# Gate and value products of a DeltaNet + SwiGLU kernel: eleven half-chunk products instead of twelve (Strassen's scheme), with weight sums streamed from DRAM

## The chip, the cores and the metric

The kernel runs on one core of one Trainium2 chip. The metric is the device time of one execution in microseconds (us); lower is better. All arithmetic and all data on the chip are 32-bit floats.

The engines are named as the profile names them: PE is the matrix engine (PEld its weight loads, which overlap its matmuls), DVE the vector engine, ACT the scalar engine, POOL the GpSimd engine, and SP the queue from which nearly all DMA transfers are issued. Every engine works through its own queue in order. [...]

## The reference

Two blocks follow each other. The first is a recurrent attention (DeltaNet); its output, regrouped to 3072 tokens of 384 features, is the input of a SwiGLU block.

```python
# q, k, v: (4, 8, 768, 48), beta: (4, 8, 768)
k_n = k / (np.linalg.norm(k, axis=-1, keepdims=True) + 1e-06)
state = np.zeros((B, H, D, D))
for t in range(S):
    y[:, :, t] = einsum('bhd,bhde->bhe', q[:, :, t], state)
    v_old = einsum('bhde,bhd->bhe', state, k_n[:, :, t])
    state = state + beta_t * einsum('bhd,bhe->bhde', k_n[:, :, t], v_t - v_old)
x = y.transpose(0, 2, 1, 3).reshape(B * S, H * D)          # 3072 x 384
g = x @ w_gate                                             # 384 -> 1536
out = (g * (1 / (1 + np.exp(-g))) * (x @ w_val)) @ w_out   # 1536 -> 384
```

## The kernel before, in words

The 768 time steps are cut into 12 chunks (`NCH`) of 64 steps. With four batches, a chunk has 256 tokens (`TOK`). For each chunk the attention makes a tile `xts[c]` of 3 x 128 features by 256 tokens, and the SwiGLU block then consumes it:

- `gate_val(c, f)` makes two blocks of 128 hidden units (`f` and `f+1`) of gate and of value. Each is a sum over three feature tiles (`t`), with 128 x 128 weights as the stationary operand and all 256 tokens as the moving operand. `p_gate` and `p_val` fill one PSUM bank each, and four banks rotate through `ps_ffn`. ACT forms `sil` = silu(`p_gate`), DVE multiplies it by `p_val` into a hidden tile `h_f`. It is called six times per chunk.
- `output_fast(c)`, from chunk 3 on (`FAST`), makes the output product with Strassen's scheme: 7 products for 8 on two halves of the hidden units, tokens and output columns. Some of its weight sums were put in place of weights that are no longer needed (`combos`), and `sums_of_h` makes sums of hidden tiles on DVE.

Chunks 0 to 2 use the plain `output`. Their weights arrive while they run: `convert` turns the inputs' 64-bit words into 32-bit floats.

The attention of the next chunk is woven into this stream of matmuls by hand, in program order:

- `point(c + 1)` emits the next small step for chunk c+1 or a later one: one of the four steps of `advance` (the recurrence, with 64 x 64 matmuls; the second step also loads `vin`, the third `kn`), a step of `products` (first the DVE transposes of k and q in `turned`, with the loads of the next blocks, then the Gram products in `gram`), or a step of `join`.
- `fill(n)` emits up to n steps of `invert(g)`, the inversion of a pair of chunks' 32 x 32 triangles on DVE. It opens with three transposes (`turn`), has one operation on POOL for which two calls are skipped (`WAIT`), goes on with 31 steps of two vector operations (`substitute`, lines 488 and 494), and closes with three more transposes and some small ones.
- `finish(c + 1)` emits whatever is left of the next chunk's steps at the end of a chunk.

So for each chunk the program has a fixed sequence: `point`, then six times [`gate_val` with `fill(2)`, `point`, `fill(3)`], then the output with `fill` and `point` between its products.

Of the kernel before, what the change touches and what calls it, by code (L numbers as in the profile page):

```python
# [20 lines left out]
def kernel(  # L21
# [51 lines left out]
    def ps_ffn(shape, name):  # L73
        return psum.tile(shape, FP32, name=name, tag="ffn", bufs=4)
# [9 lines left out]
    last_k = const.tile([128, 2 * KW], FP32, name="last_k")  # L84
    knp.append(last_k[:, 0:KW])
    kts.append(last_k[:, KW : 2 * KW])
    knp = [t.rearrange("p (bp h d) -> p bp h d", bp=NB, h=H) for t in knp]

    def slot(c):
        return c if c < AHEAD else (c - AHEAD) % (AHEAD - 1)  # L90

    def freed_by_k(c):

        return c - AHEAD if c < 2 * AHEAD - 1 else c - AHEAD + 1
# [21 lines left out]
    def load_k(c, dmas=(nc.sync,)):  # L116
        for n in range(2 * NB):
            bp, b = divmod(n, 2)
            dmas[n % len(dmas)].dma_start(  # L119
                out=knp[slot(c)][64 * b : 64 * b + 64, bp, :, 0:D],  # L120
                in_=halves(k, c, bp, b).rearrange("h p d -> p h d"),
            )
# [10 lines left out]
    K_BLOCKS, Q_BLOCKS = 6, 3  # L133
# [88 lines left out]
    def stage(n):  # L222
        _, src, t, f0, m = pieces[n]
        name, lo = place_of[n]
        if name not in places:
            tag_bufs = {"zb": 1, "p_sb": 2}[name]
            places[name] = work.tile(
                [128, 2 * PIECE], U32, name="staged", tag=name, bufs=tag_bufs
            )
        place = places[name][:, lo : lo + 2 * m]  # L230
        staged[n] = place
        nc.sync.dma_start(
            out=place, in_=src[t * 128 : (t + 1) * 128, f0 : f0 + m].bitcast(U32)
        )
# [71 lines left out]

    state = const.tile([128, 2, NB, NJ, D], FP32, name="state")
# [80 lines left out]
    def turned(c, of_q, tag=None):  # L388

        tag = tag or ("py" if of_q else "px")  # L390
        x = qpad[c % QB] if of_q else knp[slot(c)]
        if of_q:
            xt = work.tile([128, NB * NJ * 2 * C], FP32, name="qt", bufs=1)
        else:
            xt = kts[slot(c)]
        if c >= blocks_of[of_q][1]:
            xt_v = xt.rearrange("p (bp b j i) -> p bp j b i", bp=NB, b=2, j=NJ)
            (qt if of_q else kt)[c] = xt_v
            blocks = blocks_of[of_q][2]
            nc.vector.transpose(xt, blocks.rearrange("p bp h d -> p (bp h d)"))  # L400
            if c + 1 < NCH:
                load_blocks(of_q, c + 1)
            return
        xt = xt.rearrange("p (bp j b i) -> p bp j b i", bp=NB, j=NJ, b=2)
        (qt if of_q else kt)[c] = xt
        p_t = banks("p_t", tag)
        for bp in range(NB):
            for j in range(NJ):
                at = slice(128 * j, 128 * j + 128)
                nc.tensor.transpose(p_t[bp][:, at], x[:, bp, 2 * j : 2 * j + 2], ident)  # L410
        for bp in range(NB):
            nc.scalar.copy(xt[:, bp].rearrange("p j b i -> p (j b i)"), p_t[bp])
        if of_q and c + QB < Q_BLOCKS:
            load_q(c + QB)

    def gram_steps(c, of_q, tag=None, copies=(nc.vector.tensor_copy,) * 2):
# [10 lines left out]
        if of_q:  # L427
            p_sb[c] = work.tile([128, 2, NB, NJ, C], FP32, name="p_sb", bufs=2)
        elif c % 2 == 0:
            a = work.tile([128, C * 2 * HH], FP32, name="a_sb")  # L430
            a_sb[c // 2] = a.rearrange("p (c h i) -> p c h i", c=2, h=HH)
            a_of[c // 2] = a
# [139 lines left out]
    def late_z(g, zb):  # L572

        nc.vector.transpose(
            ztp[g % ZB].rearrange("p c h i -> p i (c h)")[:, R:C],
            zb.rearrange("p k i -> p i k"),
        )
        yield
        z_late[g] = work.tile([128, R, 2 * HH], FP32, name="d_t", tag="p_sb", bufs=2)
        nc.vector.transpose(z_late[g], zb)  # L580
        yield
# [126 lines left out]
    def advance(c):  # L708

        kn = knp[slot(c)]  # L710
# [58 lines left out]
        def of_state():  # L769
# [14 lines left out]
            for later in range(AHEAD, NCH):  # L784
                if freed_by_k(later) == c:
                    load_k(later)
# [29 lines left out]
    hs = {}  # L816

    def gate_val(c, f, fill, within=None, behind=None):

        ps = {}  # L820
        for w_sb, name in ((wg_sb, "p_gate"), (wv_sb, "p_val")):
            ps[name] = ps_ffn([128, 2, TOK], name)
            for i in range(2):
                for t in range(KT):
                    nc.tensor.matmul(  # L825
                        ps[name][:, i],
                        w_sb[:, t, (f + i) * 128 : (f + i + 1) * 128],
                        xts[c][:, t],
                        start=(t == 0),
                        stop=(t == KT - 1),  # L830
                    )
            if name == "p_gate":
                sil = ffn_pool.tile([128, 2, TOK], FP32, name="sil", bufs=1)
# [4 lines left out]
        at = len(hs) if c < 2 else (len(hs) - 12) % 8  # L838
        hs[c, f] = hp[at].rearrange("p (i n) -> p i n", i=2)
        nc.vector.tensor_tensor(out=hs[c, f], in0=sil, in1=ps["p_val"], op=ALU.mult)  # L840
        if c >= FAST:
            if f >= FT // 2:
                sums_of_h(c, f)
            elif combos:
                combos.pop(0)()
# [4 lines left out]
    def output(c, bp, fill, between=()):  # L850
        p_o = ps_ffn([128, DM], "p_o")
# [46 lines left out]

    def minus_t4():
        minus(w_t4[0], w_quarter(1, 0)[:, 0 : FH - 2], w_t2[:, 0 : FH - 2])  # L900
        minus(w_t4[1], w_quarter(1, 0)[:, FH - 2 : FH], w_t2[:, FH - 2 : FH])
# [28 lines left out]
    def output_fast(c, fill):  # L930

        p = {}

        def product(x, part, a, b):
            begun = (x, part) in p
            if not begun:
                p[x, part] = ps_ffn([128, DH], "p_o")
# [10 lines left out]
        def add(out, a, b):  # L948
            nc.vector.tensor_tensor(out=out, in0=a, in1=b, op=ALU.add)  # L949

# [3 lines left out]
        o = [new_o() for _ in range(NB)]  # L954
        left, right = slice(0, DH), slice(DH, DM)
        product(0, 0, lambda f: h_of(c, f, 0), quarter(0, 0))
        nc.scalar.copy(o[0][:, right], p[0, 0])
        product(0, 1, lambda f: s_of(2, f), lambda f: w_t2[:, f])
        add(o[0][:, right], o[0][:, right], p[0, 1])
        fill(2)  # L960
        product(1, 0, lambda f: h_of(c, f, 1), lambda f: w_t3[:, f])
        add(o[1][:, right], o[0][:, right], p[1, 0])
# [7 lines left out]
        add(o[1][:, right], o[1][:, right], p[1, 1])  # L970
# [7 lines left out]
        add(o[1][:, left], o[0][:, right], p[1, 0])  # L978
        store(c, 1, o[1])
        product(1, 1, lambda f: h_of(c, f + FH, 0), quarter(1, 1))  # L980
        add(o[0][:, right], o[0][:, right], p[1, 1])
        store(c, 0, o[0])
        fill(7)
# [25 lines left out]
    def products(k_c, q_c):  # L1009
# [6 lines left out]
        if k_c is not None:  # L1016
            copies = nc.scalar.copy if k_c < 6 else nc.vector.tensor_copy
            gram(k_c, False, None, (copies, copies))
# [24 lines left out]

    def prep_step(c):
# [17 lines left out]
        elif not (c > 0 and hold and not todo and k_of and steps("advance", freed_by_k(k_of[0])) >= 4):  # L1062
            return False
        if k_of and steps("advance", freed_by_k(k_of[0])) >= 4:
# [49 lines left out]
    with tc.manual_schedule(  # L1114
# [120 lines left out]
        for c in range(2, NCH):  # L1235
            point(c + 1)
            for f in range(0, FT, 2):
                gate_val(c, f, fill, behind=c + 1)
            if c >= FAST:
                output_fast(c, fill)  # L1240
            else:
                output(c, 0, fill)
                point(c + 1)
                output(c, 1, fill)
            finish(c + 1)

# [29 lines left out]
```

## Time and profile before

| | us |
|---|---|
| median of 8 runs | 735.09 (734.15 to 736.3) |
| the profiled execution: its time | 734.88 |
| the profiled execution: span from first to last instruction | 733.0 |
| PE busy, and share of the span | 697.2 (95%) |
| PE weight loads busy | 604.0 (82%) |
| DVE busy | 447.8 (61%) |
| ACT busy | 167.3 (23%) |
| POOL busy | 51.9 (7%) |
| mean granted PE clock | 0.966 |

The profile is one execution, recorded by the hardware. In its group rows a line of the source, an engine, an operation and its tiles stand first, then the shape and the count; after the bar come the busy time, the mean duration of one instruction in ns, and the idle time of the engine before them. Matmuls overlap in a pipeline, so the mean duration of one is longer than the distance from one to the next; the distance is read from the timeline or from the chain of waits. A matmul call of the kernel on 32-bit data appears as two pairs of weight load and matmul: the 72 calls of line 825 in each of the 12 chunks stand as 864 + 864 instructions. A transpose on PE (lines 410 and 805) is one pair.

### The profile page before, as it was taken

Reading aid. Unit: us, or ns where it says so; the run is one execution under the profiler, and the core shown is the slowest. Engines: PE = TensorE matmul, PEld = TensorE weight load, DVE = VectorE, ACT = ScalarE, POOL = GpSimd, SP = SyncE. Lnnn points to the kernel's source line nnn. Section 1 sums busy time; section 2 is a strip of 40 time slices with the busy share of each in tenths; the row PEclk is TensorE's granted clock in tenths of the full one; section 3 lists DMA queues with packets and bytes.
Section 4 is the critical chain, followed back from the end, with each engine's and each line's share of the span. In section 5 each row is a group of like instructions: output and inputs, shape, how many; then the busy total and the mean of one; then the engine's idle time right before and its main releaser. Section 6 shows DMA issues by size and latency. Waiting matters only on the chain.

```text
span 733.0 us, 22491 instructions
## 1 busy us (share of the span) xinstructions
PE 697.2 (95%) x10132; PEld 604.0 (82%) x10132; DVE 447.8 (61%) x904; ACT 167.3 (23%) x323; POOL 51.9 (7%) x46
## 2 busy tenths in 40 slices
PE   4657999999999999999999999999999999999997
PEld 3545888856787789988888988888988988989987
DVE  5995766697598162769853669853669853313122
ACT  3477654202401202021012021012011012021010
POOL 7003000203000000030000030000030000000000
PEclk9557999999999999999999999999999999999999
DMA  7786453210231112422102332202211000000000
GB/s 148 169 236 175 107 138 115 36 31 16 54 46 24 23 23 45 61 51 37 30 3 46 42 70 29 38 3 43 46 25 23 22 3 3 22 3 0 23 1 21
DMA packets 130736, 37.19 MB, mean 51 GB/s; under 512 B 122864, under 2 KB 125936, under 8 KB 130640
## 3 DMA queue, kind: packets, MB, share of 16 engines
q1 hardware_dynamic: 127184, 34.01, 23.0%
q10 hardware_dynamic: 3072, 1.57, 1.0%
q8 instruction: 79, 1.29, 0.8%
q0 software_dynamic: 384, 0.17, 0.1%
q14 instruction: 17, 0.14, 0.1%
HBM read 31.01 MB, written 4.72 MB: 49 GB/s over the span
## 4 chain that ended last, share of the span: by engine, by line
PE 81%; DVE 7%; SPq 3%; DMA 3%; ACT 3%; issue 2%; ACTq 0%; DVEq 0%
PE p_gate L825 24%; PE p_val L825 24%; PE p_o L939 14%; PE p_o L856 6%; PE p_g L422 2%; DVE tmp L488 2%; PE p_r L720 2%; PE p_u L741 2%; DVE zb L494 2%; PE p_s L772 1%; PE p_y L760 1%; PE p_y L729 1%; DMA zt<-in_moe_w_gate_dram 1%; SPq L127 1%; SPq L119 1%
## 5 line engine op out<-in xcount | busy, mean ns | idle before, releaser
L825 PE MATMUL p_gate<-x_ffn,wg_sb 128*128 128x256 f32 x864 | 204.5, 387 | 1.3 <-ACT x_ffn L808 1.3
L825 PE MATMUL p_val<-x_ffn,wv_sb 128*128 128x256 f32 x864 | 198.6, 379 | 0.0
L825 PEld LDWEIGHTS p_val<-x_ffn,wv_sb 128*128 128x128 f32 x864 | 163.8, 190 | 22.3
L825 PEld LDWEIGHTS p_gate<-x_ffn,wg_sb 128*128 128x128 f32 x864 | 161.2, 191 | 24.1 <-ACT x_ffn L808 1.8
L840 DVE TENSOR_TENSOR h_f<-sil,p_val 128x512 f32<-128x512 f32 x71 | 48.5, 684 | 158.5 <-PE p_val L825 156.7
L834 ACT ACTIVATE sil<-p_gate 128x512 f32<-128x512 f32 x72 | 43.0, 597 | 294.8 <-PE p_gate L825 273.1
L939 PE MATMUL p_o<-wo_sb,h_f 128*128 128x192 f32 x432 | 75.7, 328 | 1.0 <-DVE o_sb L949 0.9
L939 PEld LDWEIGHTS p_o<-wo_sb,h_f 128*128 128x128 f32 x432 | 70.2, 190 | 2.4 <-DVE o_sb L949 1.9
L488 DVE TENSOR_TENSOR tmp<-zb,mb 128x31 f32<-128x31 f32 (+15 forms) x186 | 63.4, 341 | 12.3 <-PE p_j L608 6.7
L494 DVE TENSOR_TENSOR zb<-zb,tmp 128x31 f32<-128x31 f32 (+15 forms) x186 | 63.7, 343 | 6.4
L633 POOL TENSOR_TENSOR n_b<-mb,half 128x32 f32<-128x32 f32 x5 | 28.1, 5628 | 412.2 <-DVE mb L458 372.7
L949 DVE TENSOR_TENSOR o_sb<-o_sb,p_o 128x192 f32<-128x192 f32 x45 | 15.6, 350 | 53.0 <-PE p_o L939 35.9
L856 PE MATMUL p_o<-wo_sb,h_f 128*128 128x384 f32 x136 | 45.7, 490 | 0.0
L856 PEld LDWEIGHTS p_o<-wo_sb,h_f 128*128 128x128 f32 x136 | 25.3, 190 | 16.5
L939 PE MATMUL p_o<-last_k,h_f 128*128 128x192 f32 x180 | 32.7, 328 | 1.1 <-DVE o_sb L949 1.1
L939 PEld LDWEIGHTS p_o<-last_k,h_f 128*128 128x128 f32 x180 | 29.6, 190 | 2.0 <-DVE o_sb L949 1.7
L897 DVE TENSOR_TENSOR h_f<-h_f,h_f 128x256 f32<-128x256 f32 x54 | 22.4, 424 | 8.0 <-PE p_o L939 7.1
L939 PE MATMUL p_o<-last_h,h_f 128*128 128x192 f32 x144 | 26.3, 326 | 0.0
L939 PEld LDWEIGHTS p_o<-last_h,h_f 128*128 128x128 f32 x144 | 23.9, 190 | 0.0
L741 PEld LDWEIGHTS p_u<-vin,zt 64*64 64x64 f32 x768 | 13.7, 141 | 5.6 <-issue 3.2
L458 DVE STREAM_TRANSPOSE mb<-a_sb 32x1024 f32<-32x1024 f32 x8 | 17.0, 2126 | 0.2
L752 ACT COPY uu<-p_u 128x768 f32<-128x768 f32 (+1 forms) x13 | 9.7, 750 | 31.7 <-PE p_u L741 31.7
(180 smaller groups left out, 681.3 us busy)
## 6 DMA issues: line engine op xcount, KB each, us to landing
vin<-in_v_dram SPq DMA_DIRECT2D x96, 48.0 KB
kn<-in_k_dram SPq DMA_DIRECT2D x40, 96.0 KB
out_dram<-o_sb SPq DMA_DIRECT2D x36, 96.0 KB
zt<-in_moe_w_out_dram SPq DMA_DIRECT2D x6, 384.0 KB
staged<-in_moe_w_out_dram SPq DMA_DIRECT2D x6, 384.0 KB
qpad<-in_q_dram SPq DMA_DIRECT2D x36, 64.0 KB
wo_sb<-in_moe_w_gate_dram SPq DMA_DIRECT2D x4, 512.0 KB
wo_sb<-in_moe_w_val_dram SPq DMA_DIRECT2D x4, 512.0 KB
```

Source lines behind the costliest of these rows:

```text
L458: nc.vector.transpose(out(rows, 0), in_(rows, 0))
L488: nc.vector.tensor_tensor(out=t_v, in0=zb[:, 0 : j + 1, j : j + 1].to_broadcast([128, j + 1, m]), in1=mb[:, j : j + 1, j + 1 : R].to_broad ...
L494: nc.vector.tensor_tensor(out=zb[:, 0 : j + 1, j + 1 : R], in0=zb[:, 0 : j + 1, j + 1 : R], in1=t_v, op=ALU.add,)
L633: nc.gpsimd.tensor_tensor(out=n, in0=mb.rearrange("p j i -> p (j i)")[:, 0 : R * R : R + 1], in1=half, op=ALU.pow,)
L741: nc.tensor.matmul(p_u[half_of(b), par, bp, j], zt[half_of(b ^ par), par, bp, j], r[half_of(b ^ par), par, bp, j], start=first, stop=True, ...
L825: nc.tensor.matmul(ps[name][:, i], w_sb[:, t, (f + i) * 128 : (f + i + 1) * 128], xts[c][:, t], start=(t == 0), stop=(t == KT - 1),)
L834: nc.scalar.activation(sil, ps[name], ACTF.Silu)
L840: nc.vector.tensor_tensor(out=hs[c, f], in0=sil, in1=ps["p_val"], op=ALU.mult)
L856: nc.tensor.matmul(p_o, hs[c, f - f % 2][:, f % 2, bp * 128 : (bp + 1) * 128], wo_sb[:, f], start=(f == 0), stop=(f == FT - 1),)
L897: nc.vector.tensor_tensor(out=out, in0=a, in1=b, op=ALU.subtract)
L939: nc.tensor.matmul(p[x, part], a(f - f % 2)[:, f % 2], b(f), start=not begun and f == 0, stop=f == FH - 1, skip_group_check=True,)
L949: nc.vector.tensor_tensor(out=out, in0=a, in1=b, op=ALU.add)
```

## The change

From chunk 3 on, `gate_val` is replaced by `gate_val_fast`, called three times per chunk (rounds r = 0, 1, 2). A round covers the hidden blocks f1, f1+1 and f1+6, f1+7 (f1 = 2r), for gate and value at once: four 128 x 128 blocks (`u`), the four quarters of one PSUM bank. The first two feature tiles, the two hidden blocks and the two halves of the tokens form a 2 x 2 x 2 product that Strassen's scheme (in Winograd's form) does with 7 products; the third feature tile needs 4 plain ones. A product is four matmul calls with 128 tokens as the moving operand, so a round has 11 products where 12 would be the plain count.

- Sums of weights: `sums_of_w` forms them on DVE in chunk 2. Three tiles of 128 x 512 per round are written to DRAM; each is loaded again into one of three places `w_s` through the SP queue, one round ahead, as soon as the round's product has used the place (`next_sums`). One difference of weights stays where the weight was.
- Sums of tokens: `sums_of_x` forms four 128 x 128 tiles on DVE for each chunk, by `x_sums`, in the output of the chunk before or at its end.
- Sums of products: in each round ACT copies three PSUM tiles of 128 x 512 (two of them into PSUM), and DVE adds two of that size into PSUM. Matmuls then accumulate on top of what was copied or added. Silu and the multiplication run on quarters of a round (128 x 256) instead of on whole tiles.
- The four PSUM banks are fixed (`ffn_banks`) and named by the round (`p_x`, `p_w`, `p_y`, `p_v`). `output_fast` uses the same ones; ACT clears two of them.
- The order of the woven work: a round has `fill(1)`, `point`, `fill(3)` in its middle and `point`, `fill(3)` at its end; in the output `fill(7)` becomes `fill(5)`. The two places of the weight sums are the hidden tiles 6 and 7, so hidden tiles no longer alternate over eight places. k rows get two places, transposed k four (`kn_of`, `kt_of`), and `k_ready` lets a k chunk start about one chunk earlier. From k chunk 6 on the Gram copies (`a_sb`) are on ACT instead of DVE.

```diff
+    w_s = {1: units(hp[6]), 2: units(hp[7]), 4: units(p_places[0][:, 0:512])}
+    m5 = units(p_places[0][:, 512:1024])
+    kept = {
+        (n, r): dram.tile([128, 4, 128], FP32, name=f"w_s{n}_{r}")
...
+    def sums_of_w(f):
+        if 2 <= f <= 6:
+            r = f // 2 % 3
+            f1, f2 = 2 * r, 2 * r + 6
+            for n in (1, 2, 4):
+                for m in range(2):
+                    s_ = w_s[n][:, 2 * m : 2 * m + 2]
+                    if n == 1:
+                        plus(s_, w_pair(m, 0, f2), w_pair(m, 1, f2))
+                    elif n == 2:
+                        minus(s_, w_s[1][:, 2 * m : 2 * m + 2], w_pair(m, 0, f1))
+                    else:
+                        minus(s_, w_pair(m, 1, f1), w_s[2][:, 2 * m : 2 * m + 2])
+                nc.sync.dma_start(out=kept[n, r], in_=w_s[n])
+        if f >= 6:
+            for m in range(2):
+                minus(w_pair(m, 0, f), w_pair(m, 0, f - 6), w_pair(m, 0, f))
+    def sums_of_x(c):
+        left, right = slice(0, 128), slice(128, 256)
+        b1, b2 = xts[c][:, 0], xts[c][:, 1]
+        minus(x_t[:, 0], b1[:, right], b1[:, left])
+        minus(x_t[:, 1], b2[:, right], x_t[:, 0])
+        minus(b1[:, right], b2[:, right], b1[:, right])
+        minus(x_t[:, 2], b2[:, left], x_t[:, 1])
...
+    def gate_val_fast(c, r, fill):
...
+        def product(p, w, moving, start=False):
+            for u in range(4):
+                nc.tensor.matmul(
+                    p[:, u], w(u), moving, start=start and u == 0, stop=True,
+                    skip_group_check=True,
+                )
...
+        def next_sums(n):
+            if c < NCH - 1 or r < ROUNDS - 1:
+                nc.sync.dma_start(out=w_s[n], in_=kept[n, (r + 1) % ROUNDS])
+        def begin(r):
+            product(p_x, plain(0, 2 * r), x[:, 0, tok[0]], True)
+            nc.scalar.copy(p_y, p_x)
...
+        if r == 0:
+            begin(0)
+        product(p_w, summed_w(1), x_t[:, 0], True)
+        nc.scalar.copy(m5, p_w)
+        next_sums(1)
+        product(p_y, summed_w(2), x_t[:, 1])
+        nc.scalar.copy(p_v, p_y)
+        next_sums(2)
+        product(p_x, plain(1, f1), x[:, 1, tok[0]])
+        product(p_x, plain(2, f1), x[:, 2, tok[0]])
+        plus(p_y, p_y, m5)
+        product(p_v, plain(0, f2), x[:, 0, tok[1]])
+        silu(p_x, 0)
+        fill(1)
+        times(p_x, 0, f1, 0)
+        plus(p_w, p_v, m5)
+        point(c + 1)
+        if combos:
+            combos.pop(0)()
+        else:
+            fill(3)
+        product(p_y, summed_w(4), x[:, 1, tok[1]])
+        next_sums(4)
+        product(p_y, plain(2, f1), x[:, 2, tok[1]])
+        silu(p_y, 1)
+        times(p_y, 1, f1, 1)
+        product(p_w, plain(2, f2), x[:, 2, tok[1]])
+        silu(p_w, 0)
+        times(p_w, 0, f2, 1)
+        product(p_v, plain(1, f2), x_t[:, 2])
+        product(p_v, plain(2, f2), x[:, 2, tok[0]])
+        silu(p_v, 1)
+        sums_of_h(c, f2)
+        times(p_v, 1, f2, 0)
+        if r < ROUNDS - 1:
+            begin(r + 1)
+        point(c + 1)
+        fill(3)
...
-            copies = nc.scalar.copy if k_c < 6 else nc.vector.tensor_copy
-            gram(k_c, False, None, (copies, copies))
+            gram(k_c, False, None, (nc.scalar.copy, nc.scalar.copy))
...
-            for f in range(0, FT, 2):
-                gate_val(c, f, fill, behind=c + 1)
             if c >= FAST:
+                for r in range(ROUNDS):
+                    gate_val_fast(c, r, fill)
                 output_fast(c, fill)
             else:
+                for f in range(0, FT, 2):
+                    gate_val(c, f, fill, behind=c + 1)
...
             finish(c + 1)
+            x_sums(c + 1)
```

## The prediction

> **What bounds the kernel now.** I read the page first, then the windows chunk by chunk, the chain of waits in the last chunk, the timelines of PE, DVE and SP, and the waits.
>
> The windows begin where chunks 5 to 11 begin (PE, PEld, DVE, ACT, POOL busy, clock, DMA share, GB/s):
>
> ```profile
> 358.70:414.70 56.00, 56.00 (x940) 50.36 (x938) 28.95 (x53) 8.84 (x15) 0.00 (x0) 1.00 0.15 27
> 414.70:469.80 55.10, 54.08 (x690) 48.16 (x683) 45.46 (x94) 7.24 (x13) 6.58 (x3) 1.00 0.32 48
> ...
> 684.00:729.00 45.00, 44.90 (x230) 40.88 (x228) 10.80 (x24) 4.22 (x8) 0.00 (x0) 1.00 0.05 10
> ```
>
> PE is busy in all of every chunk, at the full clock. DVE has 29 us of work in one chunk and 45 in the next: the inversion of a pair of chunks runs in every second one. So a chunk's time is the sum of PE's distances, as long as nobody keeps PE waiting. Those distances stand in the chain of the last chunk, where nothing is woven in (start, us, what; x12 counts six calls, two instructions each):
>
> ```profile
> 684.17 2.59 PE p_gate L825 x12
> 686.76 2.59 PE p_val L825 x12
> ...
> 715.25 13.66 PE p_o L939 x84
> ```
>
> 2.59 us for 12 instructions is 215.8 ns for 256 moving columns; 13.66 for 84 is 162.6 ns for 192. The slope is 0.83 ns per column, with 2.5 ns on top. Twelve pieces of 2.59 make 31.1 us of gate and value per chunk.
>
> **Products of 128 tokens.** A fast chunk had 144 instructions of 215.8 ns; it gets 3 rounds x 11 products x 4 calls x 2 = 264 of 128 columns. No stream of such matmuls is in the trace, but the six transposes of a chunk have this size, and an ordinary weight load follows them (timelines of PE, then PEld):
>
> ```profile
> 659.34 0.82 PE L805 MATMUL p_f<-ident,y 128*128 128x128 f32 x6
> 659.99 0.38 PE L825 MATMUL p_gate<-x_ffn,wg_sb 128*128 128x256 f32 x1
> ```
>
> ```profile
> 659.34 0.58 PEld L805 LDWEIGHTS p_f<-ident,y 128*128 128x128 f32 x5
> 659.88 0.30 PEld L825 LDWEIGHTS p_gate<-x_ffn,wg_sb 128*128 128x128 f32 x2
> ```
>
> Six take 0.82 us and the last one alone 0.273 (median on that line), so they are (0.82 - 0.273) / 5 = 109.4 ns apart; the slope above gives the same. The weight load for `p_gate` starts at 659.88, beside the last transpose, and its matmul follows at 659.99: the ordinary load fits too, with about a nanosecond to spare. Upper bounds: 162.6 ns, the stream of 192 columns, whose moving side alone explains it; and 116.3, twice the pace at which 64-column loads repeat in one place of the array (line 729 on the chain: 64 in 0.93 us, so 14.5 ns apart, over four places 58.1). I take 109.4, as that row has the size and the load. A chunk then needs 264 x 0.1094 = 28.9 us and saves 2.2; nine chunks (3 to 11) save 19.8. With 116.3 they save 3.5.
>
> [...]
>
> **What the round adds for PE to wait on.** I number a round's products in program order: P1 (`p_w`), P2 (`p_y`), P3 and P4 (`p_x`), P5 (`p_v`), P6 and P7 (`p_y`), P8 (`p_w`), P9 and P10 (`p_v`), P11 (the next round's first, `begin`). Each lasts 0.875. ACT starts 0.04 after a matmul's recorded end, which is 0.16 after the next product began, and PE takes up work 0.05 after its releaser ended (a DVE sum that ended at 465.05 let a load start at 465.10); the first load is then uncovered, 0.1.
>
> P2 needs ACT's copy of P11: 0.20 + 0.60 + 0.05 + 0.11 = 0.96 after P1 began, where P1 covers 0.875. So 0.08 per round, 27 rounds: +2.2. No row has ACT or DVE writing to PSUM; 0.60 is `sil` (128x512, line 834). At 0.4 it is hidden, at 0.9 it costs 10. I take the row's value. [...]
>
> DVE per round: two adds of 0.68 (line 840, also 128x512 with PSUM), four multiplications at about 0.41 (between 0.35 for 192 and 0.68 for 512 columns), three `sums_of_h` of 0.42: 4.3 us, where the two f pairs had 1.4 + 1.3. Token sums add 4 x 0.28 per chunk, and 1.3 leaves with the Gram copies on ACT. That is about +5 per chunk, on 29 or 45 of what becomes about 53. In between stand seven `fill` steps; at their largest:
>
> ```profile
> 446.80 0.42 DVE L488 TENSOR_TENSOR tmp<-zb,mb 128x247 f32<-128x247 f32 x1
> 447.25 0.42 DVE L494 TENSOR_TENSOR zb<-zb,tmp 128x247 f32<-128x247 f32 x1
> 447.58 0.68 DVE L840 TENSOR_TENSOR h_f<-sil,p_val 128x512 f32<-128x512 f32 x1
> ```
>
> A step is 0.85 here, so 5.95 for seven and 10.25 for DVE's round, against 9.63 for PE's. The woven steps help: per chunk they give PE 9.3 us and DVE 7.2. Before, four rotating banks let DVE be some 5 us late for nothing; now PE follows it closely. The add into `p_y` stands behind the last multiplication and the `fill(3)` of the round before: 0.6 + 0.41 + 2.55 + 0.68 = 4.2 after P10, while P11 and P1 to P5 cover 5.25. The add into `p_w` stands behind `fill(1)` and a multiplication: 0.85 + 0.41 + 0.68 = 1.9, covered by P6 and P7, 1.75. P1 waits for the multiplication of P8, behind the middle `fill(3)`; P9 to P11 cover it within 0.2. So these are just hidden, and not when a fill is three transposes of 2.1. Walking the queues through a pair of chunks with an inversion, I get 2.3 us lost in the chunk with the large steps and 0.7 in the one with the closing transposes. Three inversions (of chunks 6 to 11) fall into fast chunks: 9. The trace of before loses about 1.6 per inversion in its output:
>
> ```profile
> 465.11 1.57 PE L939 MATMUL p_o<-last_k,h_f 128*128 128x192 f32 x8 [0.55 <-DVE o_sb L949]
> ...
> 467.79 2.22 PE L939 MATMUL p_o<-wo_sb,h_f 128*128 128x192 f32 x12 [0.47 <-DVE o_sb L949]
> ```
>
> These 5 are within the 9, so net +4, between 0 and 15.
>
> **Chunk 2.** `sums_of_w` is 24 vector operations of 0.42, 10 us on DVE, plus nine stores. DVE's queue there ends at 238.3 and the next chunk's first multiplication finds it idle:
>
> ```profile
> 253.15 0.69 DVE L840 TENSOR_TENSOR h_f<-sil,p_val 128x512 f32<-128x512 f32 x1 [14.90 <-PE p_val L825]
> ```
>
> Of the 14.9 us the work takes 10, but `join` at 246.4 needs the end of the inversion, then at 248.3: +2, between 0 and 5.
>
> **The loads of weight sums.** Per round three of 256 KB; issuing one costs SP 0.43 (line 232, same size), and they stand behind whatever SP is issuing:
>
> ```profile
> 390.95 6.21 SPq L167 DMA_DIRECT2D vin<-in_v_dram  x8
> 397.25 3.62 SPq L119 DMA_DIRECT2D kn<-in_k_dram  x4
> 410.46 4.04 SPq L153 DMA_DIRECT2D qpad<-in_k_dram  x8
> 414.59 6.27 SPq L153 DMA_DIRECT2D qpad<-in_q_dram  x8
> ```
>
> A place is free after its product and wanted one round later, 8.8 us plus woven steps (some 12). `vin` or `kn` ahead of it fits. The 10.3 us of `turned` don't, but by the order of points they fall at the end of round 1 or later, where the loads are for the next chunk and the output's 13.66 covers them; only in chunk 3 do they come in round 0. +1.5, once. Bandwidth is no issue at a DMA share of 0.05 to 0.32.
>
> **Sum.** 734.9 - 19.8 + 2.2 + 4 + 2 + 1.5 = 724.8 for an execution like the profiled one, which is 0.2 below the median of the runs: 725.0.
>
> **Rivals.** (1) DVE binds while inversions run, and the change is slower. Place: the 18 rounds of chunks 3 to 8; mechanism: the add into `p_y` or a multiplication comes late in each round, because DVE, in order, waits for ACT and PE ahead of its fill steps and can't catch up. It decides from 0.8 us per round ((10.1 + 4) / 18); at 1.2 it is 21.6 in place of 4: 742.6. For it: 10.25 against 9.63. Against: the fills are shorter on average (two groups of 63 us for 186 steps, 0.68 a step), and over a pair of chunks DVE's sum is 29 + 45 + 10 of 106 us. (2) Weight loads bind at 116.3 ns: 264 x 6.9 ns x 9 = 16.4 more, 741.4; no gain left from 113.7. Against: the load beside the transpose. (3) SP is late in each of chunks 3 to 8, by 3 us: 18 in place of 1.5, 741.5. (4) Every wait but P2's is covered: 717.5.
>
> **How the numbers follow.** The forecast has 0.56, with a range of its own of 717 to 733; (1) 0.20, (2) 0.07, (3) 0.06, (4) 0.11. The range 715 to 741 takes in (4) with a shorter copy, the upper ends of the waits, and the milder half of (1) to (3). A measurement can tell 0.2%, 1.5 us, from no change: faster 0.73 (the forecast, (4), and a little of (1) to (3)), same 0.05, slower 0.22.
>
> **What would show it.** Right: the new products 109 ns apart, 28.9 us per chunk for them, the last chunk some 43 long instead of 45, PE waits on ACT's copy of about 0.1 per round, waits on DVE only in chunks 3 to 8. Wrong: products 114 ns or more apart throughout; PE waiting on DVE in every round, also in chunks 9 to 11 where nothing is filled in; PE waiting for DMA into `w_s`.

## The result, and the profile after

| | before | after |
|---|---|---|
| median, us | 735.27 (734.15 to 736.71, 33 runs) | 738.59 (737.1 to 740.33, 12 runs) |
| profiled execution: time, span | 734.88, 733.0 | 741.4, 739.7 |
| PE, DVE, ACT busy in it | 697.2, 447.8, 167.3 | 689.6, 498.8, 233.1 |

The ratio is 1.0043 with a 95% interval of 1.0035 to 1.0051: the change makes the kernel slower by 3.3 us, where 10 less was forecast. PE is busy for 7.6 us less, and the time goes up: PE is kept waiting.

A table of chunk lengths, worked out from the starts of each chunk's first gate matmul in PE's timeline (the last one ends where the last matmul starts), shows where. Its rows are the kernels whose chunks are compared below, by the labels of the experiments (e1 to e12); c2 starts at the time in the first column.

| kernel | start | c2 | c3 | c4 | c5 | c6 | c7 | c8 | c9 | c10 | c11 |
|---|---|---|---|---|---|---|---|---|---|---|---|
| before | 188.9 | 58.7 | 56.0 | 55.1 | 56.0 | 55.1 | 56.0 | 52.8 | 55.1 | 50.3 | 44.6 |
| after | 191.6 | 64.0 | 58.2 | 54.1 | 55.9 | 63.2 | 50.8 | 57.1 | 50.8 | 46.5 | 43.1 |
| e3 | 189.0 | 58.7 | 59.8 | 54.1 | 55.8 | 63.4 | 50.8 | 57.1 | 50.8 | 46.5 | 43.1 |
| e4 | 191.1 | 63.8 | 56.7 | 60.0 | 55.1 | 56.8 | 52.2 | 54.0 | 50.8 | 46.5 | 43.1 |
| e6 | 188.7 | 64.1 | 59.6 | 54.1 | 55.8 | 62.3 | 50.8 | 55.5 | 50.8 | 46.5 | 43.1 |
| e8 | 190.3 | 59.0 | 57.9 | 53.9 | 55.1 | 56.8 | 52.2 | 54.0 | 50.8 | 46.5 | 43.1 |
| e5 | 190.2 | 58.7 | 56.9 | 58.3 | 58.6 | 59.8 | 56.1 | 58.8 | 52.4 | 48.0 | 44.6 |
| e9 | 189.9 | 58.7 | 56.0 | 53.9 | 56.0 | 53.9 | 56.0 | 52.8 | 55.1 | 50.3 | 44.6 |
| e10 | 190.1 | 65.1 | 55.0 | 51.8 | 59.1 | 55.2 | 59.9 | 55.8 | 60.1 | 51.6 | 43.1 |
| e11 | 189.5 | 57.4 | 59.4 | 53.9 | 53.8 | 54.3 | 58.0 | 50.0 | 54.4 | 46.5 | 43.1 |

Chunks 2 to 11 together went from 539.7 to 543.6: +3.9, the loss in the median. The 2.7 by which the start of this profile is longer is its own: the profiled execution is that much above the median too. The earlier k chunks also move work from chunk to chunk (chunk 7 is 5.2 shorter, chunk 6 is 8.1 longer), so single chunks are best compared between kernels of the same order.

The last chunk, where nothing is woven in, shows what the products are worth. The chain of waits of the changed kernel in its last chunk (start, us, what) answers to the two pieces of 2.59 and the one of 13.66 of before:

```profile
692.31 29.57 PE ffn L912 x264
721.88 13.67 PE ffn L1109 x84
```

264 matmuls in 29.57 us are 112 ns apart (in the timeline 1503 distances are 112 and 757 are 111 ns, mean 111.7), not 109.4. The chunk saves 1.5, not 2.2. (e5 below has the same order of work without the products; its chunks 9 and 10 are longer by the same 1.5.)

In chunks 2, 6 and 8 the saving is eaten. The waits of PE in the changed kernel (waiting instruction, releaser: us in total, times, longest; those of the start left out):

```profile
PE ffn L1109 <- DVE o_sb L1063: 5.5, 2, 4.8
PE p_u L762 <- DVE vin L758: 4.9, 2, 3.1
...
PE ffn L912 <- DMA h_f<-w_s: 1.8, 2, 0.9
```

From chunk 2 on only two pairs are large, and neither is a product of the new rounds that waits for its own add (these come to 1.4). The timeline of chunk 2 (start, us, engine, line, what, and in brackets the idle time before it and its releaser):

```profile
225.50 0.42 DVE L1060 TENSOR_TENSOR wv_sb<-wv_sb 128x256 f32<-128x256 f32 x1
225.84 0.95 DVE L398 TENSOR_TENSOR vin<-vin,n_t 128x768 f32<-128x768 f32 x1
226.89 0.95 DVE L758 TENSOR_TENSOR vin<-vin,p_r 128x768 f32<-128x768 f32 x1
...
227.90 1.15 PE L762 MATMUL p_u<-vin,zt 64*64 64x48 f32 x64 [3.11 <-DVE vin L758]
```

The last of `sums_of_w` end just ahead of the two operations on `vin`, for which `p_u` waits 3.11. In chunk 6 it is POOL's power (pow) that DVE waits for, with an add of the output behind it:

```profile
468.69 5.44 POOL L654 TENSOR_TENSOR n_b<-mb,half 128x32 f32<-128x32 f32 x1 [81.04 <-DVE mb L479]
...
474.16 0.90 DVE L662 TENSOR_SCALAR n_b<-n_b 128x32 f32<-128x32 f32 x1 [4.72 <-POOL n_b L654]
...
480.03 0.62 DVE L1063 TENSOR_TENSOR o_sb<-o_sb,ffn 128x192 f32<-128x192 f32 x2
...
480.44 4.21 PE L1109 MATMUL ffn<-wo_sb,h_f 128*128 128x192 f32 x12 [4.81 <-DVE o_sb L1063]
```

The kernel before has this wait of DVE too, 2.1 to 2.5 us in its chunks 4, 6 and 8, but at a place where PE does not stand still for it. In chunk 8 the closing transpositions of an inversion stand ahead of `vin`:

```profile
538.46 3.95 DVE L479 STREAM_TRANSPOSE zt<-zb 32x1024 f32<-32x1024 f32 x2
...
544.15 0.95 DVE L758 TENSOR_TENSOR vin<-vin,p_r 128x768 f32<-128x768 f32 x1
...
545.16 1.15 PE L762 MATMUL p_u<-vin,zt 64*64 64x48 f32 x64 [1.78 <-DVE vin L758]
...
548.53 1.06 PE L912 MATMUL ffn<-x_ffn,wv_sb 128*128 128x128 f32 x4
```

The last line holds a second cost: four products last 1.06 there where four last 0.61 in undisturbed stretches. With each of these three waits PE falls to half its pace (in chunk 2 matmuls 427 ns apart for 215.8, in chunk 6 320 for 162.6, in chunk 8 213 for 111.7). The granted clock shows it: 0.95 over chunk 6 and 0.50 in a stretch of it, where the last chunk has 1.00 (columns as in the windows above; the clock is the third number from the end):

```profile
423.66:486.90 63.24, 57.28 (x1064) 55.47 (x1058) 50.48 (x101) 16.39 (x34) 6.58 (x3) 0.95 0.29 65
478.50:485.30 6.80, 4.86 (x40) 4.42 (x43) 3.57 (x13) 0.00 (x0) 0.00 (x0) 0.50 0.13 29
692.15:735.21 43.06, 43.06 (x348) 43.06 (x348) 15.86 (x35) 10.86 (x25) 0.00 (x0) 1.00 0.16 47
```

In chunks 2 and 8 the clock is halved for 3.4 us (from 229.3 and from 546.75), in which PE works: half of it, 1.7, is lost. In chunk 6 it is halved for 6.8 us; PE stands for the first 2 and works for 4.9, of which 2.4 are lost.

| chunk | stand of PE (distance over the usual) | half pace | together |
|---|---|---|---|
| 2 | 3.3, and 0.4 at 218.3 behind earlier sums | 1.7 | 5.4 |
| 6 | 5.0 | 2.4 | 7.4 |
| 8 | 1.9 | 1.7 | 3.6 |

### The profile page after: what moved, and what is told of

Same layout as the page of the kernel before. It is cut to its first block, busy times and chain, and to the rows that moved or that the text cites. A ratio compares the mean times of both kernels' runs of the same rounds, so it can differ in the third digit from the quotient of the medians.

```text
span 739.7 us, 25231 instructions
## 1 busy us (share of the span) xinstructions
PE 689.6 (93%) x11212; PEld 634.3 (86%) x11212; DVE 498.8 (67%) x1060; ACT 233.1 (32%) x488; POOL 51.9 (7%) x46
## 3 DMA queue, kind: packets, MB, share of 16 engines
q10 hardware_dynamic: 3072, 1.57, 1.0%
## 4 chain that ended last, share of the span: by engine, by line
PE 76%; DVE 13%; issue 3%; ACT 2%; DMA 2%; SPq 2%; POOL 1%; ACTq 0%; DVEq 0%
PE ffn L912 32%; PE ffn L1109 15%; PE ffn L992 10%; PE ffn L1019 6%; DVE tmp L509 2%; DVE zb L515 2%; PE p_g L441 2%; SPq L169 2%; PE p_u L762 2%; PE p_s L793 2%; DVE zt L479 2%; PE p_y L781 1%; PE p_r L741 1%; DVE mb L479 1%; PE p_f L826 1%
## 5 line engine op out<-in xcount | busy, mean ns | idle before, releaser
L912 PE MATMUL ffn<-x_ffn,wg_sb 128*128 128x128 f32 x756 | 117.1, 278 | 0.2 <-DVE ffn L1063 0.2
L912 PE MATMUL ffn<-x_ffn,wv_sb 128*128 128x128 f32 x756 | 115.7, 276 | 0.0
L912 PEld LDWEIGHTS ffn<-x_ffn,wg_sb 128*128 128x128 f32 x756 | 100.5, 193 | 0.8 <-DVE ffn L1063 0.4
L912 PEld LDWEIGHTS ffn<-x_ffn,wv_sb 128*128 128x128 f32 x756 | 100.1, 193 | 0.0
L1109 PE MATMUL ffn<-wo_sb,h_f 128*128 128x192 f32 x432 | 77.5, 334 | 5.5 <-DVE o_sb L1063 5.5
L1109 PEld LDWEIGHTS ffn<-wo_sb,h_f 128*128 128x128 f32 x432 | 71.9, 194 | 6.4 <-DVE o_sb L1063 6.0
L509 DVE TENSOR_TENSOR tmp<-zb,mb 128x31 f32<-128x31 f32 (+15 forms) x186 | 63.2, 340 | 11.7 <-PE p_j L629 6.7
L515 DVE TENSOR_TENSOR zb<-zb,tmp 128x31 f32<-128x31 f32 (+15 forms) x186 | 63.8, 343 | 6.4
L912 PE MATMUL ffn<-x_t,h_f 128*128 128x128 f32 x432 | 54.5, 279 | 2.1 <-DMA h_f<-w_s 1.8
L992 PE MATMUL ffn<-x_ffn,wg_sb 128*128 128x256 f32 x216 | 54.3, 404 | 1.4 <-ACT x_ffn L829 1.4
L912 PEld LDWEIGHTS ffn<-x_t,h_f 128*128 128x128 f32 x432 | 50.9, 191 | 3.1 <-ACT p_sb L949 1.1
L992 PE MATMUL ffn<-x_ffn,wv_sb 128*128 128x256 f32 x216 | 49.9, 380 | 0.0
L992 PEld LDWEIGHTS ffn<-x_ffn,wg_sb 128*128 128x128 f32 x216 | 42.5, 202 | 8.3 <-ACT x_ffn L829 1.9
L992 PEld LDWEIGHTS ffn<-x_ffn,wv_sb 128*128 128x128 f32 x216 | 40.7, 190 | 5.5
L1019 PEld LDWEIGHTS ffn<-wo_sb,h_f 128*128 128x128 f32 x136 | 25.3, 190 | 16.5
```

The source lines that it names most:

```text
L509: nc.vector.tensor_tensor(out=t_v, in0=zb[:, 0 : j + 1, j : j + 1].to_broadcast([128, j + 1, m]), in1=mb[:, j : j + 1, j + 1 : R].to_broad ...
L515: nc.vector.tensor_tensor(out=zb[:, 0 : j + 1, j + 1 : R], in0=zb[:, 0 : j + 1, j + 1 : R], in1=t_v, op=ALU.add,)
L912: nc.tensor.matmul(p[:, u], w(u), moving, start=start and u == 0, stop=True, skip_group_check=True,)
L992: nc.tensor.matmul(ps[name][:, i], w_sb[:, t, (f + i) * 128 : (f + i + 1) * 128], xts[c][:, t], start=(t == 0 and (i == 0 or c < 2)), stop ...
L1019: nc.tensor.matmul(p_o, hs[c, f - f % 2][:, f % 2, bp * 128 : (bp + 1) * 128], wo_sb[:, f], start=(f == 0), stop=(f == FT - 1),)
L1109: nc.tensor.matmul(p[x, part], a(f - f % 2)[:, f % 2], b(f), start=not begun and f == 0, stop=f == FH - 1, skip_group_check=True,)
```

## The experiments

Theory: the products gain 14; the loss is three places where DVE, in order, has something long ahead of what PE needs (waits of 3.11, 4.81 and 1.78 us). Rival: DVE (or SP) has too much to do everywhere, or the loss lies in another part of the change.

**What bounds a product (e1).**

```
-  p[:, u], w(u), moving
+  p[:, u, 0:112], w(u), moving[:, 0:112]
```

> Each of the 264 products' matmuls of a fast chunk moves 112 columns in place of 128 (16 tokens of each half are left out); the 128x128 weight loads stay. Theory: the stream is bound by its weight loads, 106.7 + 5 ns, so the distance stays at 111.7 ns and 264 of them still take 29.5 us in the last chunk. Rival: the moving columns with a fixed part bind it, 0.83 ns each; then the distance falls by 13.3 ns to some 98 and the 264 take 26 us.

In the chain of the last chunk the 264 take 111.8 ns each, where they took 112.0:

```profile
690.01 29.52 PE ffn L912 x264
```

Sixteen columns less change nothing (29.52 us for 29.57), so the moving columns don't bind the stream and the rival is out. What stays the same at 112 columns is the weight load, so it is the likely bound; no run changes the loads themselves, and a fixed time per call is not excluded. The theory's 106.7 ns are an estimate, 128 times the 0.83 ns per column of the prediction; no run shows a load of that length. The profiles fit the load: in the changed kernel's the record of a product's load lasts 0.19 us, that of the load of a transpose of the same size 0.14, and the transposes repeat at 109.2 ns.

**The streaming (e2).**

```
 def next_sums(n):
-    if c < NCH - 1 or r < ROUNDS - 1:
+    if False:
```

> The weight sums are not streamed: the three places keep the sums of round 0, which rounds 1 and 2 then use too (their own sums are left out). Theory: the streaming costs PE its two waits on DMA into the places in chunk 3 (0.9 us each) and little else, since no later chunk waits for a load; so 738.6 - 2 = 736.5, and the losses in chunks 2, 6 and 8 stay. Rival: the streamed transfers also slow the rest (SP's queue, DMA contention) and the kernel falls to 731 or less.

739.27, ratio to before 1.006 [1.0025, 1.0095]: nothing gained, so the theory's 2 us were a miss. The waits on DMA are gone, but chunk 3 stays at 58.2: one product later in the same round now waits 2.1 us for DVE's add. The rival, which had streaming slow the rest, gets nothing either: no cost of the loads shows within this interval.

**Loads from ACT's queue (e6)** is the same question with the loads kept.

```
-    nc.sync.dma_start(out=w_s[n], in_=kept[n, (r + 1) % ROUNDS])
+    nc.scalar.dma_start(out=w_s[n], in_=kept[n, (r + 1) % ROUNDS])
```

> The loads of weight sums are issued by ACT in place of SP, right behind the copy that waits for the same product. Theory: in chunk 3 they no longer stand behind SP's block loads of k and q, so the two waits on DMA (0.9 each) go and chunk 3 is 56.3 in place of 58.1; the rest stays, 738.6 - 2 = 736.6. Rival: an issue costs ACT 0.4 us or more ahead of its copies and activations, three per round, and PE then waits for ACT in each round: 27 times 0.3, 746.

737.78, 1.0036 [1.0021, 1.0051]: not clear of the changed kernel's own interval. Chunk 3 is not shorter but 1.5 longer (59.6), since the half pace followed in it this time (8 matmuls in 2.08, the last line below, where 8 take 1.06 at 280.80). Its timeline shows what the DMA wait had covered:

```profile
282.69 4.29 DVE L479 STREAM_TRANSPOSE mb<-a_sb 32x1024 f32<-32x1024 f32 x2
...
287.01 0.70 DVE L1063 TENSOR_TENSOR ffn<-ffn,p_sb 128x512 f32<-128x512 f32 x1
...
287.76 2.08 PE L912 MATMUL ffn<-x_ffn,p_sb 128*128 128x128 f32 x8 [2.14 <-DVE ffn L1063]
```

The add stands behind the opening transpositions. The rival, ACT late in every round, did not come: an issue takes ACT 0.33, and chunks 9 to 11 keep their lengths. (Chunk 8 is 55.5 for 57.1. These 1.6 us are about the 1.7 that the half pace cost there in the changed kernel, so most likely it did not follow this time.)

**The weight sums of chunk 2 (e3).**

```
-        if c == FAST - 1:
-            sums_of_w(f)          # in gate_val
...
+            if c == FAST - 1:     # behind output(c, 1)
+                sums_of_w(0)
             finish(c + 1)
             x_sums(c + 1)
+            if c == FAST - 1:
+                sums_of_w(1)      # each round into places of its own
+                sums_of_w(2)
```

> The 24 vector operations of the weight sums leave the gate and value part of chunk 2: round 0's go behind its output, those of rounds 1 and 2 behind the token sums of chunk 3, into six places of their own, so that none waits for a store. Theory: chunk 2's 5.3 us are the wait of p_u's products on the subtraction into vin behind the sums (3.1) and the half clock behind that wait (1.9); chunk 2 is then 59 us long in place of 64.0 and the kernel 738.6 - 5 = 733.6. Rival: the sums only move and are waited for at the first round of chunk 3; then chunk 3 grows by what chunk 2 loses and the time stays at 738.

735.05, 0.9991 [0.9978, 1.0005]: 3.5 less than after. Chunk 2 is 58.7, the length of before, so its 5.3 us are explained. Chunk 3 takes back 1.7: its two waits on DMA into `w_s` come to 1.9, the longer to 1.0 (1.8 and 0.9 in the changed kernel); that the half pace followed them this time is likely by the size, not shown. The sums themselves are not waited for.

**The pauses of the inversion (e4).**

```
-    WAIT = 2
+    WAIT, LONG = 2, 3
     ...                       # turn: each of its transpositions
-    yield
+    yield LONG
     ...                       # after POOL's pow
     yield WAIT
     yield WAIT
+    yield WAIT
     ...                       # fill_some
-    for _ in range(n):
+    while n > 0:
+        n -= 1
         did = next(fills[0][1], 0)
+        n -= did == LONG
```

> Only the weave of the inversion changes: one more step's pause behind POOL's pow, and each large transposition counts as two fill steps. Theory: chunk 6 loses 7 us because DVE, in order, waits 4.7 us for the pow in the output, with the add that PE waits for behind it, and chunk 8 loses 3.7 because the closing transpositions stand ahead of the subtraction into vin; both go, with the half clock behind them: chunk 6 at 56 in place of 63.2, chunk 8 at 53 to 54 in place of 57.1, the kernel at 738.6 - 10 = 728.5. Rival: DVE has too much work per round, so the waits come back in other rounds; then chunks 3 to 8 together lose as much as before and the time stays above 735.

735.18, 0.9994 [0.9978, 1.0009]. Chunks 6 and 8 are 56.8 and 54.0, as expected; the size is not, for chunk 4 has grown from 54.1 to 60.0. SP's and PE's timelines there:

```profile
316.54 5.14 SPq L169 DMA_DIRECT2D qpad<-in_k_dram  x8
321.78 5.10 SPq L169 DMA_DIRECT2D qpad<-in_q_dram  x8
326.98 0.91 SPq L926 DMA_DIRECT2D h_f<-w_s  x2
...
331.06 2.16 PE L913 MATMUL ffn<-x_t,h_f 128*128 128x128 f32 x9 [4.33 <-DMA h_f<-w_s]
```

The weave has shifted, and the block loads of k and q now stand ahead of the weight sums in a middle round. Here SP's queue does cost: 4.5 and the half pace (9 matmuls in 2.16, where 8 take 1.16 at 319.09).

**The three repairs together (e8)**: the edits of e3, e4 and e6.

> The three edits together: sums late and in places of their own, one more pause and large transpositions counted twice, loads of sums issued by ACT. Theory: each loss goes with its cause; chunks 2 to 11 take 58.7, 55.5, 54, 55, 56.8, 52.2, 54, 50.8, 46.5 and 43.1, together 526.6 where the changed kernel has 543.6; 738.6 - 17 = 721.6, against 735.3 before. Rival: PE and DVE stay so close that other waits open, and only half of it comes: 730.

725.73 (725.53 to 727.75), 0.9874 [0.9856, 0.9893]: the fastest of all, 12.9 less than after. The edits alone gave 3.5, 3.4 and 0.8 (the last not clear of noise), together 7.7. The other 5.2 are for the most part chunk 4's, which e4 had lengthened by 5.9 and which is back at 53.9: the wait on DMA there is gone, most likely by ACT's queue, though no run has e4 and e6 alone. What PE still waits for from chunk 2 on is small, by the waits of this kernel:

```profile
PE ffn L914 <- DVE ffn L1063: 1.4, 3, 0.8
...
PE p_u L763 <- DVE vin L759: 1.3, 1, 1.3
```

It missed the expected 721.6 by 4, of which 2.4 are in chunk 3. A stand of 1.7 (`p_f` waits for ACT's `y`) comes just ahead of its chunk 2; that is in e4 too.

**One pause more (e11).**

```
     mb = new_mb()
+    yield WAIT
     yield from turn(
```

> The repaired kernel with one more pause, ahead of the first large transposition of an inversion, so that in chunk 7 none stands ahead of the subtraction into vin. Theory: the wait of 1.5 us in chunk 7 goes and no other comes, 725.7 - 1.5 = 724.2. Rival: the inversions shift by a fill and another subtraction or add is then behind one: 725.7 or more.

728.89, 0.991 [0.9894, 0.9925]: the rival. The wait in chunk 7 for `vin` is gone, but two stands on DVE's adds (1.0 and 1.35) have come in the same chunk, which is 58.0. Each shift of the weave moves the waits.

**The half pace by itself (e7).**

```
+    for _ in range({9: 6, 10: 7, 11: 11}.get(c, 0)):
+        plus(sil, sil, sil)
     plus(o[1][:, right], o[0][:, right], p[1, 0])
```

> In the outputs of chunks 9, 10 and 11, which wait for nobody, 6, 7 and 11 vector operations on sil (its values are destroyed, the token sums of nothing else change) are put ahead of the add that frees the bank of the output's sixth product, so that PE stands still for some 1.0, 1.8 and 4.7 us. Theory: a stand of about 1 us costs only itself, one of 1.8 and more is followed by matmuls at half the pace (325 ns in place of 162.5) for about 3.4 us, which costs 1.7 more: chunk 9 at 51.8, chunk 10 at 50.0, chunk 11 at 49.4, against 50.8, 46.5 and 43.1. Rival: the half pace in chunks 2, 6 and 8 came from elsewhere; then only the stands themselves are added.

The theory's figures are those of the changed kernel: a stand of 1.15 in chunk 6 without the half pace, and the one of 1.78 in chunk 8 with the clock at 0.50 for 3.41 us, of which half, 1.7, is lost.

In chunks 9 and 10 the dummies (0.72 each) were hidden, so those two points were not tested. Chunk 11:

```profile
724.77 7.95 DVE L1063 TENSOR_TENSOR sil<-sil 128x512 f32<-128x512 f32 x11
...
733.03 2.93 PE L1109 MATMUL ffn<-last_k,h_f 128*128 128x192 f32 x8 [2.78 <-DVE o_sb L1063]
```

Eight matmuls take 2.93 where they take 1.46 otherwise. The chunk is 47.7 long instead of 43.1: 3.3 of standing and 1.3 of half pace. A wait of 2.78 made for the purpose, in a chunk that has none, brought the half pace with it.

**The rest of the change, without the products (e5).**

```
-    for r in range(ROUNDS):
-        gate_val_fast(c, r, fill)
+    for f in range(0, FT, 2):
+        gate_val(c, f, fill, behind=c + 1)
```

> The changed kernel with the gate and value of before in chunks 3 to 11 (12 products per f pair, no weight sums, no token sums); its other changes stay: the order of the k rows, where the key transposes go, the places in PSUM and the cleared banks. Theory: the losses in chunks 2, 6 and 8 and at the start come with the products, their vector work and their sums, not with the rest, so this is the kernel before, 735 within 2, with chunk 6 at some 55 to 57. Rival: the new order of the k rows and inversions makes the late chunks; then it is some 8 slower than before, 743, with chunk 6 at 63 or more.

746.61, 1.0149 [1.013, 1.0167]: the theory fell. Without products, sums and streams, the changed kernel is 11 slower than before. Chunk 5 of this kernel shows how:

```profile
364.71 4.30 DVE L479 STREAM_TRANSPOSE mb<-a_sb 32x1024 f32<-32x1024 f32 x2
...
370.10 0.95 DVE L758 TENSOR_TENSOR vin<-vin,p_r 128x768 f32<-128x768 f32 x1
...
371.11 1.15 PE L762 MATMUL p_u<-vin,zt 64*64 64x48 f32 x64 [1.53 <-DVE vin L758]
```

The same pattern, with the opening or the closing transpositions, stands in chunks 6, 7 and 8. The next run (e9) takes the order alone back:

```
 def k_ready():
-    return steps("advance", 2 if c < 8 else c - AHEAD) >= (3 if c < 8 else 1)
+    return steps("advance", c - 4 if c < 7 else c - 3) >= 4
 ...
-        fill(5)
+        fill(7)                   # behind output_fast
```

> The kernel without the products (12 per f pair, as before) once more, now with the times of before for taking the next k rows, and seven fill steps behind the output as before: on DVE the inversions, key transposes and subtractions stand in the order of the kernel before. What is left of the change is the places of k rows and keys, of PSUM and the cleared banks, and the Gram copies on ACT. Theory: the 11 us that it lost without the products come from the order alone, k rows taken some 1.75 chunks earlier, which puts the large transpositions ahead of the subtraction into vin; then this is the kernel before, 735.5 within 1.5. Rival: they come from the places or the cleared banks; then it stays at 745.

732.19, 0.9961 [0.9947, 0.9974]. So all of the loss of e5, 14.4 us, lies in the moment at which k rows are taken and in two fill steps; the places, the cleared banks and the Gram copies on ACT are together not slower but 3 faster than before. Chunks 4 and 6 have lost the 1.2 us each that PE waited in the output of before; that the 1.4 us of Gram copies that left DVE are the reason is argued, not shown.

**Products with the old order (e10)**: the same two lines in the changed kernel.

> The changed kernel, products and all, with the times of before for taking k rows and seven fill steps behind the output. A fast chunk has fewer fill steps than before (32 for 41), so an inversion ends a chunk's output, and the next chunk's first steps fall into the output and behind it. Theory: chunk 6's wait for POOL (7.2) and chunk 8's (3.7) go; the steps pressed behind the outputs of chunks 5 and 7 cost some 2.5 each; chunk 2's sums and chunk 3's loads stay: 738.6 - 10.9 + 5 = 732.7. Rival: pressed together, the steps of advance stand uncovered (each waits for ACT or DVE, with the half clock behind it) and cost 5 and more per pair: 740.

752.98, 1.0239 [1.0214, 1.0264]: the rival, and more. `join` and `advance` are pressed into the output and behind it, and the last steps stand bare, as PE's timeline at the end of chunk 5 shows (two more stands of that chunk, 1.7 and 1.9, are on DVE's adds and multiplications inside its rounds):

```profile
419.44 0.87 PE L826 MATMUL p_f<-ident,y 128*128 128x128 f32 x6 [1.57 <-ACT y L816]
...
421.21 0.71 PE L912 MATMUL ffn<-x_ffn,wg_sb 128*128 128x128 f32 x4 [0.89 <-ACT x_ffn L829]
```

The four kernels make a square: with the old order the products cost 20.8 (732.2 to 753.0), with the early one they gain 8.0 (746.6 to 738.6). The early order costs 14.4 without them and gains 14.4 with them. Neither edit can be priced alone. (The products' edit also takes nine fill steps out of each chunk, so the square does not part the products from the weave that comes with them.)

**Before, once more (e12).**

> The kernel before once more, for its start: in its profile chunk 2 begins at 188.9 us; in the ten profiles with the change, none of which touches the start, it begins between 188.65 and 191.6. Theory: the 2.6 us by which the start of the changed kernel's profile was longer differ from run to run with the waits marked issue; this one's start lies in the same band, and its chunks 2 to 11 are as in the first profile within 0.3 us. Rival: 188.9 again, and the start of the changed kernel is longer by its code.

735.26; chunk 2 begins at 189.3, the chunks are as in the first profile within 0.02 us. In the profiles of the other kernels the start lies between 188.65 and 191.6, without a pattern by edit; one more start of before cannot settle whether the change adds some tenths there.

## Why the prediction was wrong

The forecast for chunks 2 to 11 was -10.1; the profile has +3.9. Three terms of the sum were mis-sized, and the largest miss is the one for the inversions.

| step of the sum | forecast | measured |
|---|---|---|
| products | -19.8 | -14.3 |
| P2 waits for ACT's copy | +2.2 | +0.5 |
| waits on DVE in inversions | +4 | +10.6 (what is left of the +3.9) |
| chunk 2, `sums_of_w` | +2 | +5.3 |
| loads of weight sums | +1.5 | +1.8 |

- **"I take 109.4, as that row has the size and the load."** Mis-sized: 111.7. The row had the size but not the load: in the profile of before a transpose's load lasts 0.14 us and a plain product's 0.19. e1 rules the moving columns out (29.52 us with 112 of them, 29.57 with 128), which leaves the load or a fixed time per call. Rival (2) was right in kind, as far as that goes, with a third of its price (2.3 of 6.9 ns). Over nine chunks this is 5.5 us.
- **"Walking the queues through a pair of chunks with an inversion."** The largest miss, 6.6 us; with the products' 5.5 and chunk 2's 3.3 it turned the sign. The step counted DVE's work per round against PE's. DVE's total was foreseen well (51.0 us more are measured; the forecast's 5 in each of nine chunks and 10 in chunk 2 make 55); the places were not. The earlier start of the k chunks, which is part of the change, had no term in the sum: in the traces the last three inversions open in the middle of chunk 3, at the start of chunk 5 and past the middle of chunk 6, instead of at the start of chunks 4, 6 and 8. That puts the large transpositions and POOL's pow (5.44) at other places between PE's demands: pow into the output of chunk 6, the closing transpositions ahead of `vin` in chunk 8. e4, which moves only the inversions' steps, takes 6.5 and 3.1 us off chunks 6 and 8. The order is not simply dear: e5 and e9 price it at +14.4 without the products, e10 and the changed kernel at -14.4 with them.
- **"The trace of before loses about 1.6 per inversion in its output"** is a misreading. The two stands shown come to 1.35 by the distances, they are in two of the three inversions only (chunks 4 and 6), and e9, which lacks them, is 1.2 shorter in each of these. So some 2.4 was to be taken off the 9, not 5.
- **Rival (1)** saw DVE as the engine that would turn the change, and gave 742.6. Its mechanism, a little late in every round, is not there: chunks 4, 5 and 7 have 1.2 us of stands together. Three places made most of the loss.
- **"Of the 14.9 us the work takes 10."** The idle time was at the end of the chunk, but the sums stand in program order inside it, ahead of `vin`. So the 14.9 us hid none of them, and `p_u` waited 3.11; e3 puts the sums there, and PE does not wait for them (chunk 2 is 58.7, as before).
- **P2 and the loads.** In the changed kernel an ACT copy of 128x512 from PSUM (where the matmuls write `p_x`) to PSUM lasts 0.57, the one into `m5` 0.585, and PE loses 0.03 in 15 of the 27 rounds, less than the 0.08 in each. The loads come late in chunk 3 alone, as forecast; e2 and e6 show that taking them away there gains nothing, since DVE is late in the same round. Rival (3) became real only in e4's chunk 4.
- **No term for what follows a wait.** The half pace cost 5.8 in the three chunks. It lies inside the measured rows of the table, 4.1 in the inversions and 1.7 in chunk 2.

The repaired kernel comes out within 1 us of the forecast's 725.0, but by chance and not by its sum: its chunks 2 to 11 save 10.3. If the products give 14.3 and the parts of e9 2.4 there too, waits and shifted work take 6.4 back.

## What to carry over

When PE is nearly full and the side work is in a fixed order, price an edit by what stands in the queue ahead of each thing that PE waits for, not by the engine's sum of work; an edit of the order needs a line of its own in the sum. A change that shortens one stage shifts everything woven into it: here the repair of three places was worth four times the loss. Keep long operations (here transpositions of 2.1 us, a wait of 4.7 for POOL) away from the last thing ahead of a demand of PE, and, where a queue is late, consider an issuer that already waits for the same event (e6, which paid only together with e4).

## What the runs showed of the hardware

- After some waits of PE its pace was half of the usual. In the changed kernel's profile, from chunk 2 on, this came with the three longest, 4.81, 3.11 and 1.78 us, and with none of the next four, 1.15, 0.90, 0.89 and 0.65. The granted clock there is 0.50 for 3.41 us from 229.32 (1.4 after PE had resumed), for 6.83 from 478.49 (while PE still stood, 1.95 before it resumed) and for 3.41 from 546.75 (1.6 after). It cost 1.7, 2.4 and 1.7 us. In the profile of before, PE's longest wait from chunk 2 on is 0.55, and the clock is 1.00 from 188.9 to 731.5.
- In other runs, the matmuls behind a wait of PE, and the same kind without one:

| run, chunk | wait of PE | behind it | usual | half pace |
|---|---|---|---|---|
| e4, 4 | 4.33 | 9 of 128 columns in 2.16 | 8 in 1.16 | yes |
| e7, 11 | 2.78 | 8 of 192 columns in 2.93 | 8 in 1.46 | yes |
| e6, 3 | 2.14 | 8 of 128 columns in 2.08 | 8 in 1.06 | yes |
| e10, end of 5 | 1.57 | 16 of 128 columns in 1.98 | 8 in 1.06 | no |
| e5, 5 | 1.53 | 10 of 256 columns in 4.11 | 12 in 2.75 | yes |
| e8, 7 | 1.34 | 7 of 128 columns in 1.05 | 8 in 1.06 | no |

The 1.57 of e10 was not followed by it and the 1.53 of e5 was, so the length of the wait alone does not decide; what else does, no run shows.

- In each of the two profiles of before and after, the granted clock changes only at whole multiples of 3.413 us from its other changes: the three falls above are 249.17 and 68.26 us apart, 73 and 20 times as much. Why it changes at these moments no run shows.
- The changed kernel's stream of 128x128 loads and 128-column matmuls repeats at 111.7 ns, and e1's with 112 columns at 111.8. The six transposes of the same size repeat at 109.2; why their loads are quicker (0.14 us for 0.19 in the records) stays open.
- POOL's pow on 128x32 takes 5.44 us in the changed kernel, in one inversion 6.2. DVE's next operation on the same tile takes 0.17, and 0.90 where DVE has just waited for POOL.
